# Seventh unit of layer one ahead of the sixth, bank copies ahead of casts, and narrowing in other steps

## The chip, the cores and the metric

The kernel runs on one core of a Trainium2 chip, in one launch. The metric is the device time of that launch in microseconds: 2001.27 is the median of three runs (1999.72 to 2001.92). TensorE (PE in the rows) multiplies, and loads its weights beside that (PEld). VectorE (DVE), ScalarE (ACT) and GpSimd (POOL) work on tiles, and the DMA queues are issued by SyncE (SP). Each engine runs its instructions in the order in which they stand.

## The reference

Windowed attention, a mixture of eight experts weighted by a Sinkhorn normalisation, and a second feed-forward layer, all in float32:

```python
x = attention(q, k, v)                       # 2304 tokens x 512
P = exp(x @ w_gate - max); 8 rounds of row and column normalisation
for e in range(8):                           # layer one, 1024 hidden units each
    h = np.maximum(x @ w1[e], 0.0)
    out += P[:, e:e + 1] * (h @ w2[e])
h = out @ w_in                               # layer two, 2048 hidden units
r = np.maximum(h, 0.0)
return (r * r) @ w_out
```

The weights w_in and w_out come as float64 bit patterns in int64 words and have to be made float32 on the chip; the kernel calls this narrowing.

## The kernel before

**Stages.** Attention and the Sinkhorn rounds come first. Then 80 steps, each with 256 hidden units: steps 0 to 31 are pass one over the experts (tokens 0 to 1023 as a pair of 512, with tokens 1024 to 1279 as a "single"), 32 to 63 are pass two over the experts (tokens 1280 to 2303), 64 to 71 and 72 to 79 the same two passes of layer two. Numbers are float32 split in a high part (a cast to float32r, on ScalarE) and a low part (the rest, a subtraction on VectorE); a product takes three matmuls, high by high, high by low and low by high.

**Units.** The pair of a step is multiplied in Strassen's manner. Layer one has seven units u1 to u7 of six matmuls of 512 columns (`l1_pair`, lines 683 to 799), in three banks: a (shown as s), b (pt) and c (xt). u1 fills a, and ScalarE copies it to b (line 759); u2 fills c; u3 adds into a and finishes block (0,0); u4 and u5 add into b, and ScalarE copies b to s2 and to s3 (lines 771 and 775). VectorE adds bank c into s3 (line 776), which finishes block (1,1). u6 adds into b and finishes (1,0). u7 adds into c; VectorE adds c into s2 (line 785), which finishes (0,1). Each block is scaled on VectorE (line 723) into r1 (0,0), r2 (1,1), r3 (1,0) and r4 (0,1), the last two in `mix32`. The second layer of a step is done in the step behind it (`l2_mixed`, lines 929 to 1001): 14 units v10 to v71 of three matmuls, from seven operands: "11" (from r1), "22" (r2), "21" (r3), and t1 to t4, which GpSimd makes by four subtractions from r1 to r4 (`mix`, line 737). `operand` (line 700) gives each its high part by a cast (line 702) and its low part by a subtraction (line 705). v1 reads "11", v2 "21", v6 t2, v3 "22", v7 t3, v4 t4, v5 t1; the last digit is a half of the output. Between these units ScalarE copies one bank into another (`copied`, line 967), and VectorE adds finished banks into `acc` (line 957). Pass one has besides us (24 matmuls of 256 columns) and w0, w1 for the single.

**Order.** Units are issued in the order of a string `names` in the main loop (line 1249 on); pass two runs "u1 v10+v11 u2 v20 u3 v60+v50 u4+cp v51+v30+v70 u5 v21+v61 u6 v40+v71+v31 u7 v41". Each item is one tick. `after(k, f)` (line 634) puts an instruction of the other engines k ticks later, behind what is already due there. So each engine's order is fixed by these ticks, and an instruction that waits holds up all behind it.

**Narrowing and splitting.** 32 pieces of 512 x 128 words; each is loaded by DMA (`load_raw`), goes through three stages on VectorE (`narrow`, lines 312 to 338: two, two and three instructions), and is stored. `work` holds the ticks behind which a stage is issued, `loads` those of a load without a stage. Pieces below DEEP = 7 are done in pass one, in steps 22 to 28, three stages a step; those below MID = 25 in pass two, two stages a step (ticks 6 and 12); the rest later. Splits (`split_on`, `blocks_of`) prepare the next pass's input in parts, one a step: a cast (line 360) and a subtraction on VectorE (line 363). Products of the second layer go through three banks "mm".

## Time and profile before

| | |
|---|---|
| median of three runs | 2001.27 us |
| the profiled execution's own time | 2000.11 us |
| its span, first to last instruction | 1998.3 us |
| TensorE busy | 1906.1 us (95%) |
| TensorE's weight loads busy | 1545.0 us (77%) |
| VectorE busy | 1648.7 us (83%) |
| ScalarE busy | 924.2 us (46%) |
| GpSimd busy | 789.5 us (40%) |
| mean granted clock of TensorE | 0.991 of 2.4 GHz |

Busy shares are means over stages that differ. Pass one lies from about 99 to 917 us, pass two to 1609, layer two behind it. In a timeline a row gives the start, the duration, the engine, the line, what is written and read, and in brackets how long the engine was idle before and what released it. A matmul's record is longer than the distance to the next one, since matmuls overlap.

### The profile page before, as it was taken

How to read it: one execution, taken by the hardware profiler on the slowest of the kernel's cores; microseconds unless marked ns; L12 is line 12 of the kernel's file. 1: busy time of each engine (PE TensorE's matmuls, PEld its weight loads, DVE VectorE, ACT ScalarE, POOL GpSimd, SP SyncE). 2: the span in 40 equal slices, each digit the busy share in tenths (PEclk: the TensorE clock that was granted, in tenths of full speed). 3: DMA queues.
4: the chain of work that ended last, by engine and by line, in shares of the span. 5: the costliest groups of instructions: out<-in, count | busy, mean ns of one | idle time of the engine just before them, and what ended most of it. 6: DMA issues, size and time to landing. Idle time of an engine off the chain costs nothing.

```text
span 1998.3 us, 28397 instructions
## 1 busy us (share of the span) xinstructions
PE 1906.1 (95%) x10247; PEld 1545.0 (77%) x10247; DVE 1648.7 (83%) x2344; ACT 924.2 (46%) x1568; POOL 789.5 (40%) x648
## 2 busy tenths in 40 slices
PE   8999999999999999999998999999899999999998
PEld 6678788888888777787777777777777778888777
DVE  6786799989999999987688888887778798875686
ACT  6744455545554444443433433433333466553544
POOL 3522466556655455452223323322322434421231
PEclk9999999999999999999999999999999999999999
DMA  8674676766666665659666876667555788879561
GB/s 294 232 280 156 235 240 231 246 240 237 232 249 222 206 231 190 221 213 393 252 256 210 297 262 242 231 254 253 217 214 196 286 332 328 310 285 381 212 233 64
DMA packets 166205, 492.78 MB, mean 247 GB/s; under 512 B 16992, under 2 KB 36336, under 8 KB 166064
## 3 DMA queue, kind: packets, MB, share of 16 engines
q1 hardware_dynamic: 166064, 490.96, 67.8%
q8 instruction: 81, 1.33, 0.3%
q14 instruction: 60, 0.49, 0.1%
HBM read 282.15 MB, written 208.74 MB: 246 GB/s over the span
## 4 chain that ended last, share of the span: by engine, by line
PE 42%; DVE 9%; POOL 3%; issue 2%; ACT 2%; POOLq 0%; ACTq 0%; DVEq 0%
PE pt L625 10%; PE mm L946 7%; PE s L946 7%; PE mm L849 6%; PE xt L625 4%; PE s L625 4%; POOL r L735 3%; DVE g L705 3%; PE xt L946 1%; PE mm L806 1%; DVE mix L723 1%; DVE s L785 1%; ACT s L968 1%; DVE acc L957 1%; ACT g L702 0%
## 5 line engine op out<-in xcount | busy, mean ns | idle before, releaser
L735 POOL TENSOR_TENSOR r<-mix,r 128x512 f32<-128x512 f32 x67 | 87.2, 1301 | 818.2 <-DVE mix L723 723.4
L705 DVE TENSOR_TENSOR g<-r,g 128x512 fp32r<-128x512 f32 x268 | 257.3, 961 | 91.7 <-ACT g L702 85.7
L946 PE MATMUL mm<-g,w2h 128*128 128x512 f32 x670 | 213.8, 401 | 49.4 <-ACT s L968 48.7
L702 ACT CAST g<-r 128x512 fp32r<-128x512 f32 x268 | 163.3, 620 | 209.5 <-POOL r L735 109.9
L946 PE MATMUL s<-g,mixh 128*128 128x512 f32 x670 | 216.1, 399 | 12.8 <-DVE g L705 12.1
L702 ACT CAST g<-mix 128x512 fp32r<-128x512 f32 x201 | 124.3, 620 | 176.4 <-DVE mix L723 88.4
L946 PEld LDWEIGHTS mm<-g,w2h 128*128 128x128 f32 x670 | 124.2, 190 | 88.2 <-ACT s L968 63.5
L957 DVE TENSOR_TENSOR acc<-mm,acc 128x512 f32<-128x512 f32 x260 | 177.0, 681 | 4.2 <-PE mm L946 4.1
L957 DVE TENSOR_TENSOR acc<-s,acc 128x512 f32<-128x512 f32 x260 | 174.3, 682 | 6.6 <-PE s L946 6.1
L946 PEld LDWEIGHTS s<-g,mixh 128*128 128x128 f32 x670 | 125.4, 189 | 54.3 <-DVE g L705 25.7
L705 DVE TENSOR_TENSOR g<-mix,g 128x512 fp32r<-128x512 f32 x201 | 150.7, 762 | 1.4
L946 PE MATMUL mm<-g,w2l 128*128 128x512 f32 x335 | 132.5, 396 | 0.0
L849 PE MATMUL mm<-w2h,g 128*128 128x512 f32 x416 | 129.8, 393 | 0.1
L625 PE MATMUL pt<-x_hi,sumh 128*128 128x512 f32 x316 | 127.4, 403 | 1.1 <-ACT s L771 0.7
L625 PE MATMUL s<-x_hi,blkh 128*128 128x512 f32 x316 | 126.1, 399 | 0.0
L625 PE MATMUL s<-x_lo,blkh 128*128 128x512 f32 x316 | 125.3, 397 | 0.0
L625 PE MATMUL s<-x_hi,blkl 128*128 128x512 f32 x316 | 125.0, 395 | 0.0
L625 PE MATMUL pt<-x_lo,sumh 128*128 128x512 f32 x316 | 124.6, 394 | 0.0
L625 PE MATMUL pt<-x_hi,suml 128*128 128x512 f32 x316 | 124.1, 393 | 0.0
L625 PE MATMUL xt<-x_hi,sumh 128*128 128x512 f32 x316 | 123.6, 391 | 0.3 <-DVE s L776 0.3
L625 PE MATMUL xt<-x_hi,suml 128*128 128x512 f32 x316 | 123.1, 389 | 0.0
L625 PE MATMUL xt<-x_lo,sumh 128*128 128x512 f32 x316 | 123.0, 389 | 0.0
(262 smaller groups left out, 4930.3 us busy)
## 6 DMA issues: line engine op xcount, KB each, us to landing
raw<-in_w SPq DMA_DIRECT2D x61, 512.0 KB, 4.1
w_blkh<-blkh SPq DMA_DIRECT2D x40, 512.0 KB, 5.1
w_blkl<-blkl SPq DMA_DIRECT2D x40, 512.0 KB, 5.8
w_sumh<-sumh SPq DMA_DIRECT2D x40, 512.0 KB, 5.3
w_suml<-suml SPq DMA_DIRECT2D x40, 512.0 KB, 4.5
w_w2h<-w2h SPq DMA_DIRECT2D x40, 512.0 KB, 6.3
w_w2l<-w2l SPq DMA_DIRECT2D x40, 512.0 KB, 6.3
blkh<-w_blkh SPq DMA_DIRECT2D x40, 512.0 KB, 4.8
```

The lines of the kernel that those rows point to most:

```text
L625: nc.tensor.matmul(ps, w[:, c], z[:, x, j], start=start and k == 0, stop=stop and k == 5, skip_group_check=True)
L702: after(k, lambda: nc.scalar.copy(b[:, 0], src))
L705: lambda: nc.vector.tensor_tensor(out=b[:, 1], in0=src, in1=b[:, 0].bitcast(F32), op=ALU.subtract),
L723: lambda: nc.vector.scalar_tensor_tensor(out=g, in0=src, scalar=0.0, in1=p, op0=ALU.max, op1=ALU.mult),
L735: sub = lambda o, x, y: nc.gpsimd.tensor_tensor(out=o, in0=x, in1=y, op=ALU.subtract)
L785: after(0, lambda: nc.vector.tensor_tensor(out=made["s2"], in0=bank_c, in1=made["s2"], op=ALU.add))
L806: nc.tensor.matmul(ps, w[:, c], z[:, kc], start=k == 0, stop=k == len(terms) - 1)
L849: nc.tensor.matmul(ps, g[:, c0 * 128:c0 * 128 + 128], wt[:, fc], start=k == 0, stop=k == 3 * FC - 1)
L946: nc.tensor.matmul(ps, w[wt][:, c], block[n][:, g], start=start and k == 0, stop=stop and k == 2, skip_group_check=True)
L957: nc.vector.tensor_tensor(out=o, in0=ps, in1=o, op=ALU.add)
L968: after(0, lambda: nc.scalar.copy(out, src))
```

## The change

u7 and u6 change places wherever the mixing operands of the next step hang on them, so that u7 stands directly behind v21+v61, and u6 two items later. The casts and subtractions that follow are given other ticks: t1 now comes before t2, "21" and "22" later, and the subtraction r3 - r5 is issued on its own behind u6. v50 comes before v60. `copied` puts the bank copy first among what is due in its tick, not last. Narrowing: three pieces in steps 3 and 4, none in steps 22 to 28, and in pass two 22 pieces instead of 18, with two buffers in turn, at ticks 4 and 8, or 4, 6 and 8 where nothing is split. The splits of pass one move from steps 4 to 19 to steps 6 to 21. Of the table of orders two lines are shown, and of the diff what the text speaks of.

```diff
@@ -44,7 +44,7 @@
 NEG = -1e30
 NWARM = 9
 TURN = 4
-DEEP = 7
+DEEP = 3
 MID = 25
 
 
@@ -288,7 +288,7 @@
             return
         asked[0] += 1
         which, s, k = raw_pieces[n]
-        z = deep[0] if n < DEEP else raw2 if n < MID else apart[0]
+        z = deep[0] if n < DEEP else (raw2, acc[1])[n % 2] if n < MID else apart[0]
         src = loaded[n] = z.bitcast(I32).rearrange("p (n w) -> p n w", w=2)
         nc.sync.dma_start(
             src.rearrange("p n w -> p (n w)"),
@@ -728,9 +728,10 @@
                 k += 2 if i <= NS1 else 1
                 operand("11", g, k, k + 1)
             elif (fc, t) == (1, 1):
-                operand("22", g, *((7, 8) if i + 1 in first else (5, 6) if i < NS1 else (4, 5)))
+                operand("22", g, *((7, 8) if i + 1 in first else (6, 7)))
             elif (fc, t) == (1, 0):
-                operand("21", g, k + 1, k + 2 if moe else k + 3)
+                operand("21", g, 2, 3)
+                after(4, lambda: nc.gpsimd.tensor_tensor(out=r3, in0=r3, in1=r5, op=ALU.subtract))
             else:
                 sub = lambda o, x, y: nc.gpsimd.tensor_tensor(out=o, in0=x, in1=y, op=ALU.subtract)
 
@@ -738,12 +739,11 @@
                     sub(r1, r4, r1)
                     sub(r5, r2, r1)
                     sub(r4, r2, r4)
-                    sub(r3, r3, r5)
 
                 after(2, mix)
-                t1, t2, t3, t4 = ((3, 4), (4, 5), (5, 7), (6, 8)) if i >= NS1 else ((5, 7), (5, 6), (6, 9), (7, 11))
+                t1, t2, t3, t4 = ((4, 5), (5, 6), (6, 7), (8, 9)) if i >= NS1 else ((6, 7), (7, 8), (8, 10), (11, 13))
+                operand("t1", r1, *t1)
                 operand("t2", r5, *t2)
-                operand("t1", r1, *t1)
                 operand("t3", r4, *t3)
                 operand("t4", r3, *t4)
 
@@ -778,14 +778,14 @@
 
         def u6():
             product(bank_b, i, "blk", 3, 3, stop=True)
-            out(1, 0, bank_b, 1 if steps[i][0] and mixed(i) else 0)
+            out(1, 0, bank_b, 0)
+            if steps[i][0] and steps[i][1] % SPE == SPE - 1:
+                after(1, lambda: load_p(pair_of(i), steps[i][1] // SPE + 1, 1))
 
         def u7():
             product(bank_c, i, "sum", 3, 2, stop=True)
             after(0, lambda: nc.vector.tensor_tensor(out=made["s2"], in0=bank_c, in1=made["s2"], op=ALU.add))
             out(0, 1, made["s2"], 1 if mixed(i) else 2)
-            if steps[i][0] and steps[i][1] % SPE == SPE - 1:
-                after(1, lambda: load_p(pair_of(i), steps[i][1] // SPE + 1, 1))
 
         def results():
             made_here()
@@ -965,7 +965,7 @@
             after(0, f)
 
         def copied(out, src):
-            after(0, lambda: nc.scalar.copy(out, src))
+            due.setdefault(clock[0], []).insert(0, lambda: nc.scalar.copy(out, src))
 
         def chain(m, b1, b2, b3, p):
             def v1():
@@ -1249,18 +1249,20 @@
...
                 elif i < NS1:
-                    names = "u1 v10 u2 v20 w0 u3 v60+v50+v11 u4+cp v51+v30+v70 u5 v21+v61 u6 v40+v71+v31 w1 u7 v41 us"
+                    names = "u1 v10 u2 v20 w0 u3 v50+v60+v11 u4+cp v51+v30+v70 u5 v21+v61 u7 w1 v40+v71+v31 u6 v41 us"
                 else:
-                    names = "u1 v10+v11 u2 v20 u3 v60+v50 u4+cp v51+v30+v70 u5 v21+v61 u6 v40+v71+v31 u7 v41"
+                    names = "u1 v10+v11 u2 v20 u3 v50+v60 u4+cp v51+v30+v70 u5 v21+v61 u7 v40+v71+v31 u6 v41"
@@ -1268,10 +1270,10 @@
                 order = [together([(u | v)[n] for n in item.split("+")]) for item in names.split()]
                 l2, l2s, l1s, ahead = [], [], [], []
             elif i == TURN:
-                order = l2[:5] + l2s + l1[:4] + [u for k in range(3) for u in (l2[5 + k], l1[4 + k])]
+                order = l2[:5] + l2s + l1[:4] + [u for k, n in ((5, 4), (6, 6), (7, 5)) for u in (l2[k], l1[n])]
                 l2, l2s = [], []
             else:
-                for u in l1[4:]:
+                for u in (l1[4], l1[6], l1[5]) if i == first[3] else l1[4:]:
                     order += l2[:1] + [u]
                     l2 = l2[1:]
             order += l2 + l2s + l1s
@@ -1293,15 +1295,15 @@
                 splits.append(blocks_of(1, y_dram[:, :, :2 * T], y0 + raw))
             if i == 2 * NS1 - 1:
                 apart[:] = xb(), post[0].tile([128, T], F32, tag="pp", name="pp", bufs=3)
-            if i == TURN:
+            if i in (SCALED - 1, SCALED):
+                deep.append(xb())
+            if i == TURN + 2:
                 y = two(xb()) + two(xb())
                 splits.append(blocks_of(0, x_dram, y + two(mixes[0][0])))
-            if i == TURN + 17:
-                deep[:] = xb(), xb()
             if i == 2 * NS1 + 1:
                 y1 = two(mix32) + tuple(post[0].tile([128, T], F32, tag="pp", name="pp", bufs=3) for _ in range(2))
                 splits.append(blocks_of(2, y_dram[:, :, PAIRS[1]:], y1 + two(mixes[0][0]) + two(xb().bitcast(F32R))))
-            if TURN <= i < TURN + 16:
+            if TURN + 2 <= i < TURN + 18:
                 split_on(0, 8, 9)
             elif NS1 + 4 <= i < 2 * NS1 - 4:
                 split_on(1, 5, 9)
@@ -1312,10 +1314,13 @@
                 for k, f in enumerate(operands_single()):
                     after(8 + 2 * k, f)
             work, loads = (), ()
-            if TURN + 17 <= i < NS1 - 1 and done[0] < DEEP:
-                work, loads = ((), (2,)) if i == TURN + 17 else ((1, 8, 14), ())
-            elif NS1 < i < 2 * NS1 - 3 and done[0] < MID:
-                work, loads = ((), (2,)) if i == NS1 + 1 else ((6, 12), ())
+            if i == SCALED - 1:
+                loads = (3,)
+            elif SCALED <= i <= TURN:
+                work = (1, 4, 7) if i == SCALED else (1, 4, 7, 13, 15, 17)
+            elif NS1 <= i < 2 * NS1 - 3:
+                work = () if i == NS1 else (4, 8) if NS1 + 4 <= i < NS1 + 20 else (4, 6, 8)
+                loads = (15, 17) if i == NS1 else ()
             elif 2 * NS1 - 1 <= i < first[3] - 1 and done[0] < len(raw_pieces):
                 work = () if i == 2 * NS1 - 1 else (2, 4, 6)
                 loads = (8,)
```

The order that comes out in a pass-two step, first on ScalarE, around the copy from v10's bank (L968 "s<-mm"); L702 are the casts of r1 to r5, and L759 is u1's copy. In the kernel before r_2749, r_2750 and r_2751 are r1, r2 and r5, and mix_1878 holds r3 and r4. Before:

```order
L968 COPY s<-s 128x512
L702 CAST g_1875<-r_2750 128x512
L702 CAST g_1875<-mix_1878 128x512
L759 COPY pt<-s 128x512
L702 CAST g_1875<-r_2749 128x512
L968 COPY s<-mm 128x512
L702 CAST g_1876<-r_2751 128x512
L702 CAST g_1876<-mix_1878 128x512 x2
```

After; r1, r2 and r5 are r_2764, r_2765 and r_2766:

```order
L968 COPY s<-s 128x512
L702 CAST g_1875<-r_2765 128x512
L702 CAST g_1875<-r_2764 128x512
L702 CAST g_1875<-mix_1878 128x512
L759 COPY pt<-s 128x512
L968 COPY s<-mm 128x512
L702 CAST g_1876<-r_2766 128x512
L702 CAST g_1876<-mix_1878 128x512 x2
```

The cast of t1 (from r1) has moved from between the two copies to ahead of u1's copy.

On VectorE, the stretch up to the addition of s3 (L776) in a pass-two step with a split; L957 are additions into acc, L313 and L317 a first stage of narrowing, L363 a split's subtraction. Before:

```order
L705 TENSOR_TENSOR g_1876<-mix_1878,g_1876 128x512 x2
L705 TENSOR_TENSOR g_1875<-r_2749,g_1875 128x512
L313 TENSOR_SCALAR sums<-raw_113 128x512
L317 SCALAR_TENSOR_TENSOR sums<-raw_113,sums 128x512
L957 TENSOR_TENSOR acc_1873<-s,acc_1873 128x512
L957 TENSOR_TENSOR acc_1873<-mm,acc_1873 128x512
L363 TENSOR_TENSOR raw_111<-xb,raw_111 128x512
L776 TENSOR_TENSOR s_152<-xt,s_152 128x512
```

After, in which acc_1874 is the second buffer of loads:

```order
L705 TENSOR_TENSOR g_1876<-mix_1878,g_1876 128x512
L705 TENSOR_TENSOR g_1875<-r_2764,g_1875 128x512
L957 TENSOR_TENSOR acc_1873<-s,acc_1873 128x512
L957 TENSOR_TENSOR acc_1873<-mm,acc_1873 128x512
L313 TENSOR_SCALAR sums<-acc_1874 128x512
L317 SCALAR_TENSOR_TENSOR sums<-acc_1874,sums 128x512
L363 TENSOR_TENSOR raw_111<-xb,raw_111 128x512
L776 TENSOR_TENSOR s_152<-xt,s_152 128x512
```

The stage of narrowing has moved from ahead of the two additions to between them and L776.

## Rows read from the trace of the kernel before

**Rows 1.** Windows: start:end, length, each engine's busy us, clock, DMA share, GB/s.

```profile
159.00:214.80 55.80, 55.80 (x286) 47.03 (x285) 32.96 (x45) 27.39 (x41) 10.15 (x12) 1.00 0.57 195
...
617.10:642.10 25.00, 24.99 (x123) 20.85 (x123) 21.38 (x29) 12.04 (x19) 14.01 (x13) 1.00 0.66 232
667.50:867.50 200.00, 184.96 (x843) 148.44 (x842) 189.81 (x242) 85.49 (x133) 99.87 (x85) 0.97 0.62 214
917.40:1006.50 89.10, 82.89 (x355) 66.34 (x354) 61.35 (x88) 36.46 (x65) 20.49 (x14) 0.98 0.78 297
1006.50:1350.40 343.90, 317.07 (x1345) 251.30 (x1344) 288.03 (x425) 132.98 (x238) 106.94 (x72) 0.99 0.69 252
1350.40:1567.40 217.00, 199.60 (x842) 159.82 (x841) 173.38 (x256) 78.88 (x140) 59.39 (x40) 0.98 0.64 235
1567.40:1587.30 19.90, 19.51 (x85) 15.60 (x84) 15.71 (x23) 8.79 (x15) 5.97 (x4) 1.00 0.43 162
```

**Rows 2.** Waits of TensorE: who waited, for whom, total us, times, longest.

```profile
PE mm L946 <- ACT s L968: 48.7, 31, 2.2
...
PE mm L806 <- DVE acc L875: 1.9, 8, 0.3
```

**Rows 3.** Timeline, pass two, from u7's end to v20: start, duration, engine, line.

```profile
1091.09 0.69 DVE L785 TENSOR_TENSOR s<-xt,s 128x512 f32<-128x512 f32 x1 [0.67 <-PE xt L625]
...
1091.70 0.42 DVE L330 TENSOR_SCALAR raw<-sums 128x512 int32<-128x512 int32 x1
...
1092.88 0.69 DVE L336 TENSOR_TENSOR sums<-sums,raw 128x512 f32<-128x512 f32 x1
...
1094.69 0.68 DVE L723 SCALAR_TENSOR_TENSOR mix<-s,pp 128x512 f32<-128x512 f32 x1
...
1095.52 1.27 POOL L735 TENSOR_TENSOR r<-mix,r 128x512 f32<-128x512 f32 x1 [9.12 <-DVE mix L723]
...
1096.82 0.62 ACT L702 CAST g<-r 128x512 fp32r<-128x512 f32 x1 [3.12 <-POOL r L735]
...
1097.35 0.58 ACT L968 COPY s<-mm 128x512 f32<-128x512 f32 x1
1097.47 2.88 DVE L705 TENSOR_TENSOR g<-r,g 128x512 fp32r<-128x512 f32 x2 [1.49 <-ACT g L702]
...
1097.98 1.22 PE L946 MATMUL mm<-g,w2h 128*128 128x512 f32 x2 [2.17 <-ACT s L968]
```

**Rows 4.** Timeline, pass one, step 23: a stage of narrowing, then what follows it.

```profile
672.49 1.39 DVE L313 TENSOR_SCALAR xb<-xb 128x512 int32<-128x512 int32 x1 [0.70 <-DMA xb<-in_w_in]
...
675.51 1.21 DVE L705 TENSOR_TENSOR g<-r,g 128x512 fp32r<-128x512 f32 x1
...
676.77 0.50 PE L946 MATMUL s<-g,mixh 128*128 128x512 f32 x1 [1.66 <-DVE g L705]
```

**Rows 5.** Timeline, pass two, step 40: up to u6's first matmul.

```profile
1104.25 0.42 DVE L313 TENSOR_SCALAR sums<-raw 128x512 int32<-128x512 int32 x1
...
1104.71 0.69 DVE L317 SCALAR_TENSOR_TENSOR sums<-raw,sums 128x512 int32<-128x512 int32 x1
...
1106.64 0.69 DVE L957 TENSOR_TENSOR acc<-mm,acc 128x512 f32<-128x512 f32 x1
...
1107.25 0.68 DVE L363 TENSOR_TENSOR raw<-xb,raw 128x512 fp32r<-128x512 f32 x1
...
1108.62 0.69 DVE L776 TENSOR_TENSOR s<-xt,s 128x512 f32<-128x512 f32 x1 [0.69 <-ACT s L775]
...
1109.16 0.39 PE L625 MATMUL pt<-x_hi,blkh 128*128 128x512 f32 x1
```

**Rows 6.** Timeline, pass one, step 13, with a split: up to u6's first matmul.

```profile
431.06 0.85 DVE L363 TENSOR_TENSOR mixh<-xb,mixh 128x512 fp32r<-128x512 f32 x1
...
431.84 0.68 DVE L776 TENSOR_TENSOR s<-xt,s 128x512 f32<-128x512 f32 x1
431.99 0.39 PE L625 MATMUL pt<-x_hi,blkh 128*128 128x512 f32 x1
```

More of the change, by code (lines that the diff above doesn't have):

```diff
@@ L1251, in tile_kernel @@
                 if i == first[2]:
-                    names = "v10 u1 v20 us v60+v50 v51+v30 v70 u2 v11 u3 v40 u4+cp v21+v61 u5 v71+v31 u6 v41 u7"
+                    names = "v10 u1 v20 us v50+v60 v51+v30 v70 u2 v11 u3 v40 u4+cp v21+v61 u5 v71+v31 u6 v41 u7"
                 elif i == NS1:
                     u |= zip(("w0", "w1"), l2s)
-                    names = "v10 u1 v20 w0 v60+v50 w1 v51+v30 u2 v11 u3 v70 u4+cp v21+v61 u5 v40+v71+v31 u6 v41 u7"
+                    names = "v10 u1 v20 w0 v50+v60 w1 v51+v30 u2 v11 u3 v70 u4+cp v21+v61 u5 v40+v71+v31 u7 v41 u6"
                 elif i == first[1] - 1:
-                    names = "u1 v10 u2 v20 w0 u3 v11 u4 v60+v50+cp u5 v51+v30+v70 u6 v21+v61 u7 w1 v40+v71+v31 us v41"
-                elif i in (first[2] - 1, len(steps) - 1):
-                    names = "u1 v10+v11 u2 v20 u3 u4 v60+v50+cp u5 v51+v30+v70 u6 v21+v61 u7 v71+v40+v31 v41"
+                    names = "u1 v10 u2 v20 w0 u3 v11 u4 v50+v60+cp u5 v51+v30+v70 u7 v21+v61 u6 w1 v40+v71+v31 us v41"
+                elif i == first[2] - 1:
+                    names = "u1 v10+v11 u2 v20 u3 u4 v50+v60+cp u5 v51+v30+v70 u7 v21+v61 u6 v71+v40+v31 v41"
+                elif i == len(steps) - 1:
+                    names = "u1 v10+v11 u2 v20 u3 u4 v50+v60+cp u5 v51+v30+v70 u6 v21+v61 u7 v71+v40+v31 v41"
                 elif i < NS1:
-                    names = "u1 v10 u2 v20 w0 u3 v60+v50+v11 u4+cp v51+v30+v70 u5 v21+v61 u6 v40+v71+v31 w1 u7 v41 us"
+                    names = "u1 v10 u2 v20 w0 u3 v50+v60+v11 u4+cp v51+v30+v70 u5 v21+v61 u7 w1 v40+v71+v31 u6 v41 us"
                 else:
-                    names = "u1 v10+v11 u2 v20 u3 v60+v50 u4+cp v51+v30+v70 u5 v21+v61 u6 v40+v71+v31 u7 v41"
+                    names = "u1 v10+v11 u2 v20 u3 v50+v60 u4+cp v51+v30+v70 u5 v21+v61 u7 v40+v71+v31 u6 v41"
                 def together(fs):
```

## The prediction, made before the changed kernel had run

> **What bounds the kernel now.** I read the table of engines first: TensorE is busy 95% of the span, so time can be won only where it waits or runs at its lower clock. Then the windows [rows 1], cut where steps begin (at a step's first matmul of u1). A pass-one step that neither narrows nor splits takes 25.00 us and TensorE is busy for all of it. The seven steps from 667.5 us, in which layer-two weights are narrowed, take 200.0 us, 28.6 each, at a mean granted clock of 0.97 instead of 1.00, so part of them ran at 1.2 GHz. In pass two sixteen steps take 343.9 us (21.49 each) and the next ten 217.0 us (21.70 each), while the step at 1567.4 us, which narrows nothing, takes 19.90.
>
> Third, the waits [rows 2]: the largest of TensorE is 48.7 us, 31 times, for a ScalarE copy of line 968. Fourth, the timeline around one such wait [rows 3]. u7's result is added at 1091.09; the narrowing that follows u7 runs on VectorE from 1091.70 to 1093.57; only then come two low parts and the scaling (1094.69), GpSimd's subtraction (1095.52), ScalarE's cast of t1 (1096.82), and behind it in ScalarE's order the copy (1097.35 to 1097.93). v20 overwrites the bank that this copy reads, so it starts at 1097.98, after 2.17 us of idle. The copy had nothing to wait for but its place in the queue: its source was v10's bank, finished two units before.
>
> The floor of a pass-two step: 19.90 less 0.39 of idle (busy 19.51) [rows 1], less some 0.16, because a matmul's record is 0.39 us long while the next starts after about 19.9 / 85 = 0.23, so a short wait shows less idle than it costs. That gives 19.35.
>
> A sentence of the Trainium skill bears on this reading (Perfetto Trace Analysis, Identifying the Most-Contended Engine): matmul occupancy is a poor measure of headroom, and the busy share of weight loads a better one. By matmul occupancy the sixteen steps could gain 343.9 - 317.1 = 27 us; by weight loads, brought from 251.3 / 343.9 = 0.73 to the 0.83 of the clean pass-one step, 43 us, which is close to what the step times give (343.9 - 16 x 19.35 = 34); the trace sides with the page, and the sum below goes by step times.
>
> **The change part by part.**
>
> *Narrowing leaves steps 22 to 28.* The cause of the loss there is in [rows 4]: a first stage waits 0.70 us for its DMA with VectorE's whole queue behind it, its first instruction takes 1.39 us (0.42 in [rows 5]), the low part behind it ends at 676.72, and TensorE starts at 676.77 after 1.66 us of idle. The delay shows one step after the narrowing, hence the window from step 23. After the change these steps hold neither narrowing nor splits (which end at step 21), so I give them the clean 25.00: 200.0 - 7 x 25.0 = **-25.0 us**. What is late next there is u7, priced below.
>
> *Three pieces go into steps 3 and 4.* Nine stages, 1.15 us each in lines 313 and 317 [rows 5] or 1.87 for a third stage [rows 3]. In that stretch VectorE is busy for 33.0 of 55.8 us and TensorE for all of it [rows 1]; banks of products are three deep, and that covers a stage. Lower bound 0; upper, the price that the 21 stages had in pass one, 25.0 / 21 = 1.2 each, 10.7. In step 4 u7 also comes one pair of units after u5, and step 5 inherits third-stage work in front of its low parts. I take **+4**, nearer the idle VectorE than the full one.
>
> *u7 ahead of u6.* u7 adds into the bank that u5's sum s3 is read from, so it must wait for VectorE's add of line 776; u6 needed only ScalarE's copy before it. Its new place is where u6 began. In a pass-one step with a split the add runs 431.84 to 432.52 and u6 began at 431.99 [rows 6]: 0.53 late, plus 0.05 from release to matmul as in [rows 3] (1097.93 to 1097.98), about 0.6. There are 14 such steps: +8.4. Without the split's subtraction (line 363, 0.78 from its start to the add's) VectorE is ready in time, and what is left is the copy of s3 and the add behind it: 1109.31 against 1109.16 [rows 5], 0.2. Twelve steps: +2.4. In exchange w1 comes directly behind u7 and its add no longer holds the single's bank: 8 waits of 1.9 us in all [rows 2], each 0.16 more in truth, -3.2. Together **+7.6**. Behind the waiting u7 on TensorE stand w1, v40, v71, v31 and u6, all of which move with it; nobody else waits longer.
>
> The gain of the same swap: the mixing starts two units, 15 matmuls or 3.4 us, earlier, and u6's own product r3 is taken out of the chain (its subtraction moves behind the others). "21" now comes after u6, at the end of the step, and is wanted at v20: in pass two five units later, with VectorE's queue waiting there for TensorE; no cost.
>
> *Bank copies ahead of casts, and no narrowing behind u7, in pass two.* Casts of 22, t1 and 21 still stand ahead of v10's copy. t1 is ready 3.4 us sooner by the swap and 1.9 us sooner by the stage that no longer follows u7: 5.3 us against a wait of 2.17 [rows 3]. The cast of 21 needs u6, which ends one v unit and u1 before v10: 2 us for an add of 0.7 and a cast of 0.6. So the wait at v20 goes. The cover of the casts that now stand behind the copy (t2, t3) is u2, v20 and u3, 3.4 us, against 0.6 us of copy; without it each step would pay 0.6.
>
> *What is late next in pass two: u7 again.* Narrowing now stands at places 4 and 8 (steps 36 to 51) or 4, 6 and 8 (33 to 35 and 52 to 60), and place 8 is right in front of line 776 on VectorE. In [rows 5] v70's addition ends at 1107.33; a first or second stage (1.15) makes 1108.4, line 363 (0.6 net of overlap) 1109.0, the add 1109.7: 0.55 late with the release. A third stage (1.87) makes it 1.25. One stage in three is a third: mean 0.78. With three stages the split's subtraction is gone, but two stages stand ahead of v70's addition; I take the same 0.78. Bounds: 0.2, if VectorE gets ahead, and 1.5. So 25 steps x (19.35 + 0.78) + 19.55 for step 61 = 522.8 against 343.9 + 217.0 = 560.9: **-38.1 us**. The extra four pieces cost VectorE some 16 us, spread over a stretch where it is idle for 344 - 288 us; two buffers instead of one take the loads off its path.
>
> *Steps 32 to 35*: 89.1 us; step 32 has twelve matmuls more, so the floor is 4 x 19.35 + 2.7 = 80.1, and three steps narrow (0.78 each): up to -6.6, of which I take **-4**, since the turning transposes of step 32 stay. *Second pass of layer two*: seven steps at 0.2 for u7, less what the earlier mixing returns: **+1**.
>
> Sum: -25.0 + 4 + 7.6 - 38.1 - 4 + 1 = -54.5. The profiled execution took 2000.11 us, so 1945.6; the median of the runs is 1.2 us above it, so **1946 us** in round numbers.
>
> **The rivals.**
>
> *VectorE gets ahead in pass two.* Steps no longer stretched by stalls could leave it earlier at v70's addition, or stages overlap better. For: it idles 0.69 us before line 776 now [rows 5]. Against: v70's addition waits for TensorE, so its end is fixed. u7 then waits 0.2: 25 x 0.58 = 14.5 us less, 1932.
>
> *GpSimd and VectorE collide before v20 in pass one.* The mixing now runs beside the wide low parts and the low part of "21". Beside GpSimd's subtractions two low parts took 2.88 us [rows 3], where one alone takes some 0.7. From u7's end to v20 TensorE has 39 full matmuls and 24 half ones, 11.6 us; VectorE has ten operations of 0.62 and two wide ones of 1.2 to 2, about 9.3. Three stretched by 0.8 each use that up, and wide ones stretched too leave v20 0.5 to 1.5 us late: 26 steps, +13 to +39, 1959 to 1985. By the Trainium skill (SBUF — State Buffer, two separate sides) a VectorE operation with two SBUF inputs and a GpSimd operation that reads SBUF shut each other out for a whole instruction; by that rule the stretch would be a full subtraction, 1.3 to 1.7 us, and this rival the likelier, while 2.88 for two lies below two full exclusions.
>
> *Slower: u7 becomes the new bottleneck everywhere.* Without u7's waits the other terms come to about -86 us; u7 stands ahead of u6 in some 66 steps, so from 1.3 us per step the change loses. The price that could do it is a third stage and a split ahead of line 776 (1.25) plus matmuls at the lower clock after it, about 1.7: 66 x 1.7 - 86 = +26, 2027. Against: most steps have no third stage at place 8, pass one none at all.
>
> *The copy does not act*: something ahead of it in ScalarE's queue still waits, say the cast of 21. Pass two then keeps its 21.5 us, and -25 + 4 + 7.6 + 1 leaves 1989.
>
> **How the numbers follow.** Forecast (1934 to 1960) 0.63; VectorE ahead 0.15; collision 0.12; copy without effect 0.06; slower 0.04. The range for 8 in 10 takes in the forecast, the first rival down to 1926 and the cheap half of the collision, to 1970. Within 0.2% (4 us, about what a measurement of this kernel can tell from no change) only a mixture falls, 0.01; slower by more 0.04; faster by more 0.95.
>
> **What would show it.** Windows of steps 23 to 29 near 25 us each; no wait at line 968 in pass two; in its place TensorE waiting for VectorE's line 776 at the xt product of u7, 0.2 to 1.3 us a step, longest behind third stages and in pass one only with splits; granted clock 1.00 in pass two. Wrong it would be by a wait at v20 for a low part in pass one, by u7's wait over 1.3, or by steps 3 to 5 growing by more than 10 us.

## The result and the profile after

The changed kernel takes 1944.89 us (median of four runs, 1944.12 to 1945.29) against 2000.56 for the kernel before beside it: a ratio of 0.9721, with a 95% interval of 0.9704 to 0.9737. The forecast was 1946 us, in a range of 1926 to 1970. The profiled execution has a span of 1943.5 us where that of before had 1998.3. The table of engines:

```profile
PE 1888.3 (97%) x10247; PEld 1539.0 (79%) x10247; DVE 1651.7 (85%) x2344; ACT 925.2 (48%) x1568; POOL 755.1 (39%) x648
```

The windows of the changed kernel, cut again where steps begin. Columns: start and end, length, busy time (and count) of TensorE, its weight loads, VectorE, ScalarE and GpSimd, granted clock, DMA share, GB/s. In the order of the rows they are steps 3 and 4, step 22, steps 23 to 29, 32 to 35, 36 to 51, 52 to 61 and step 62; the last row is steps 6 to 21:

```profile
159.00:215.80 56.80, 55.36 (x283) 46.49 (x282) 41.94 (x60) 26.09 (x39) 11.80 (x14) 1.00 0.57 200
659.00:684.60 25.60, 25.18 (x122) 20.68 (x121) 22.90 (x29) 12.20 (x19) 13.51 (x13) 1.00 0.57 205
684.60:863.90 179.30, 176.34 (x842) 144.71 (x841) 160.28 (x197) 85.41 (x133) 94.64 (x85) 1.00 0.60 211
914.90:1002.90 88.00, 82.78 (x355) 66.34 (x354) 67.89 (x103) 35.91 (x65) 18.38 (x14) 0.98 0.85 322
1002.90:1320.70 317.80, 309.76 (x1346) 251.06 (x1345) 290.48 (x425) 134.54 (x238) 101.29 (x73) 1.00 0.73 273
1320.70:1516.00 195.30, 193.38 (x842) 156.92 (x841) 181.13 (x270) 79.53 (x140) 55.35 (x41) 1.00 0.69 261
1516.00:1535.40 19.40, 19.36 (x85) 15.56 (x84) 15.97 (x23) 8.83 (x15) 5.09 (x5) 1.00 0.56 217
...
246.90:659.00 412.10, 402.71 (x1922) 330.73 (x1921) 377.03 (x463) 202.55 (x318) 234.30 (x201) 1.00 0.65 232
```

Against [rows 1]: the seven steps from 23 fell from 200.0 to 179.3 us, the sixteen from 36 from 343.9 to 317.8, and the granted clock of both is 1.00 now. But a pass-one step that narrows and splits nothing takes 25.60 (step 22) where it took 25.00, and steps 6 to 21 take 25.76 each (412.10 / 16). TensorE is no longer busy for all of them.

The waits of TensorE (who, for whom, total us, times, longest), against [rows 2]:

```profile
PE xt L625 <- DVE s L776: 17.7, 43, 1.4
PE s L946 <- DVE acc L957: 10.7, 27, 0.8
PE mm L946 <- DVE g L705: 5.4, 3, 3.0
```

Of the 31 waits for the copy of line 968 one of 0.5 us is left, in step 32. In their place stands u7 behind VectorE's add of line 776, as forecast, and a wait that no part of the prediction names: a second-layer product into bank "s", behind an addition of line 957, 27 times. In the kernel before it occurred twice:

```profile
PE s L946 <- DVE acc L957: 1.4, 2, 0.8
```

**u7 in pass two.** VectorE in step 41, up to u7's first matmul (start, duration, engine, line; in brackets the idle time before and what ended it):

```profile
1112.85 0.69 DVE L957 TENSOR_TENSOR acc<-mm,acc 128x512 f32<-128x512 f32 x1
1113.46 0.42 DVE L330 TENSOR_SCALAR acc<-sums 128x512 int32<-128x512 int32 x1
...
1114.64 0.69 DVE L336 TENSOR_TENSOR sums<-sums,acc 128x512 f32<-128x512 f32 x1
1115.25 0.69 DVE L363 TENSOR_TENSOR raw<-xb,raw 128x512 fp32r<-128x512 f32 x1
1115.85 0.68 DVE L776 TENSOR_TENSOR s<-xt,s 128x512 f32<-128x512 f32 x1
...
1116.59 0.50 PE L625 MATMUL xt<-x_hi,sumh 128*128 128x512 f32 x1 [1.06 <-DVE s L776]
```

v70's addition, then a third stage (1113.46 to 1115.33), the split's subtraction and the add: the order in which the prediction put them. u7 starts 1.45 us after the matmul before it, where 0.23 is usual, so the step loses 1.22; with a first or second stage (step 40) the distance is 0.72 and the loss 0.49.

Why v20 doesn't wait any more: the cast of t1 starts 2.9 us after u7's add (line 787, from 1118.30) in the same step, and the copy and v20 follow in the next:

```profile
1121.19 0.62 ACT L702 CAST g<-r 128x512 fp32r<-128x512 f32 x1 [0.16 <-POOL r L736]
...
1124.44 0.57 ACT L968 COPY s<-mm 128x512 f32<-128x512 f32 x1
...
1126.28 0.61 PE L946 MATMUL mm<-g,w2h 128*128 128x512 f32 x2
```

The cast of t1 ends 2.6 us ahead of the copy, where in [rows 3] it ended at the copy's start with v20 waiting behind both.

**The new wait in pass one.** Step 14, from u7's addition to v41. v41's first half goes into bank "s" again, which the last addition here still reads:

```profile
469.83 0.69 DVE L787 TENSOR_TENSOR s<-xt,s 128x512 f32<-128x512 f32 x1 [0.51 <-PE xt L625]
...
471.19 0.75 DVE L875 SCALAR_TENSOR_TENSOR acc<-mm,ptile,acc 128x512 f32<-128x512 f32 x1 [0.67 <-PE mm L849]
...
471.86 1.22 DVE L178 TENSOR_TENSOR suml<-sums,sumh 128x1024 fp32r<-128x1024 f32 x1
...
472.99 0.69 DVE L723 SCALAR_TENSOR_TENSOR mix<-s,pp 128x512 f32<-128x512 f32 x1
...
473.59 0.68 DVE L957 TENSOR_TENSOR acc<-mm,acc 128x512 f32<-128x512 f32 x1
...
474.19 1.28 DVE L957 TENSOR_TENSOR acc<-s,acc 128x512 f32<-128x512 f32 x2
...
474.93 0.73 PE L946 MATMUL s<-g,w2h 128*128 128x512 f32 x2 [0.38 <-DVE acc L957]
```

w1 stands directly behind u7 now. Its addition (line 875) waits for its product; behind it in VectorE's order stand the wide low part of the next step's sums (1.22), the scaling of u7's block, the addition of v40, and only then that of v71, which frees the bank. Before, w1 and u7 stood behind v71 and ahead of v41, so their work on VectorE came later than that addition.

**Step 5.** One long wait is left there, behind a third stage that stands at place 17 of step 4. VectorE (and one instruction of GpSimd) up to v20, and v20:

```profile
216.50 0.92 DVE L330 TENSOR_SCALAR xb<-xb 128x512 int32<-128x512 int32 x1
...
217.46 1.67 DVE L333 SCALAR_TENSOR_TENSOR xb<-xb 128x512 f32<-128x512 uint32 x1
...
218.54 1.18 POOL L192 TENSOR_TENSOR sums<-raw 128x256 f32<-128x256 f32 x1
...
219.16 1.11 DVE L336 TENSOR_TENSOR xb<-xb 128x512 f32<-128x512 f32 x1
...
221.39 1.21 DVE L705 TENSOR_TENSOR g<-mix,g 128x512 fp32r<-128x512 f32 x1
...
222.65 0.50 PE L946 MATMUL mm<-g,w2h 128*128 128x512 f32 x1 [2.96 <-DVE g L705]
```

The stage takes 3.77 us from 216.50 to 220.27, beside subtractions of GpSimd, against 1.87 in pass two [rows 3], and the low part of "21" (221.39 to 222.60) follows two other operations. Step 5 takes 31.0 us where it took 27.2.

### The profile page after: what moved, and what is told of

Read it like the earlier page. It is cut to its first block, busy times and chain, and to the rows that moved or that the text cites. A ratio compares the mean times of both kernels' runs of the same rounds, so it can differ in the third digit from the quotient of the medians.

```text
span 1943.5 us, 28331 instructions
## 1 busy us (share of the span) xinstructions
PE 1888.3 (97%) x10247; PEld 1539.0 (79%) x10247; DVE 1651.7 (85%) x2344; ACT 925.2 (48%) x1568; POOL 755.1 (39%) x648
## 4 chain that ended last, share of the span: by engine, by line
PE 64%; DVE 26%; issue 4%; ACT 3%; DMA 2%; POOL 0%; SPq 0%; DVEq 0%; ACTq 0%; POOLq 0%
PE mm L849 11%; PE xt L625 10%; PE pt L625 9%; PE mm L946 9%; PE s L625 8%; PE s L946 8%; DVE acc L957 6%; DVE g L705 5%; PE mm L806 3%; DVE s L776 2%; DVE mixl L178 2%; PE xt L946 2%; DVE suml L178 2%; DVE mix L723 1%; DVE blkl L178 1%
## 5 line engine op out<-in xcount | busy, mean ns | idle before, releaser
L705 DVE TENSOR_TENSOR g<-r,g 128x512 fp32r<-128x512 f32 x268 | 253.3, 964 | 25.1 <-ACT g L702 23.8
L702 ACT CAST g<-r 128x512 fp32r<-128x512 f32 x268 | 165.3, 621 | 113.5 <-DVE acc L957 52.8
L946 PE MATMUL mm<-g,w2h 128*128 128x512 f32 x670 | 208.1, 391 | 7.8 <-DVE g L705 5.4
L946 PE MATMUL s<-g,mixh 128*128 128x512 f32 x670 | 206.9, 390 | 0.0
L705 DVE TENSOR_TENSOR g<-mix,g 128x512 fp32r<-128x512 f32 x201 | 190.9, 950 | 3.0 <-ACT g L702 3.0
L957 DVE TENSOR_TENSOR acc<-s,acc 128x512 f32<-128x512 f32 x260 | 172.8, 684 | 11.3 <-PE s L946 11.2
L957 DVE TENSOR_TENSOR acc<-mm,acc 128x512 f32<-128x512 f32 x260 | 177.3, 682 | 0.2 <-PE mm L946 0.2
L702 ACT CAST g<-mix 128x512 fp32r<-128x512 f32 x201 | 124.5, 620 | 107.8 <-DVE mix L723 58.6
L625 PE MATMUL xt<-x_hi,sumh 128*128 128x512 f32 x316 | 130.9, 414 | 18.7 <-DVE s L776 17.7
L246 POOL TENSOR_TENSOR raw<-raw 128x256 f32<-128x256 f32 x36 | 38.2, 1060 | 273.6 <-DVE w2l L178 249.2
L734 POOL TENSOR_TENSOR mix<-mix,r 128x512 f32<-128x512 f32 x67 | 103.0, 1538 | 95.7 <-DVE g L705 95.7
L625 PE MATMUL pt<-x_hi,sumh 128*128 128x512 f32 x316 | 123.1, 389 | 0.0
```

What stands on the lines that cost most here:

```text
L246: tt(out=r[:, 1, 1], in0=r[:, 0, 1], in1=r[:, 1, 1], op=ALU.add)
L625: nc.tensor.matmul(ps, w[:, c], z[:, x, j], start=start and k == 0, stop=stop and k == 5, skip_group_check=True)
L702: after(k, lambda: nc.scalar.copy(b[:, 0], src))
L705: lambda: nc.vector.tensor_tensor(out=b[:, 1], in0=src, in1=b[:, 0].bitcast(F32), op=ALU.subtract),
L734: after(4, lambda: nc.gpsimd.tensor_tensor(out=r3, in0=r3, in1=r5, op=ALU.subtract))
L946: nc.tensor.matmul(ps, w[wt][:, c], block[n][:, g], start=start and k == 0, stop=stop and k == 2, skip_group_check=True)
```

## Experiments

All ratios are to the kernel before, run beside it on the same chip, each from at least four runs. Lengths of steps come from one profiled execution each.

**Narrowing alone.** From the kernel before, only the narrowing and its splits and buffers are moved as in the change:

```diff
-DEEP = 7
+DEEP = 3
...
-            if TURN <= i < TURN + 16:
+            if TURN + 2 <= i < TURN + 18:
...
-            if TURN + 17 <= i < NS1 - 1 and done[0] < DEEP:
-                work, loads = ((), (2,)) if i == TURN + 17 else ((1, 8, 14), ())
...
+            elif SCALED <= i <= TURN:
+                work = (1, 4, 7) if i == SCALED else (1, 4, 7, 13, 15, 17)
+            elif NS1 <= i < 2 * NS1 - 3:
+                work = () if i == NS1 else (4, 8) if NS1 + 4 <= i < NS1 + 20 else (4, 6, 8)
```

> The kernel before with the narrowing moved as in the change (three pieces in steps 3 and 4, 22 in pass two with two buffers at ticks 4, 8 or 4, 6, 8, splits two steps later); u6 ahead of u7, bank copies last. Theory 1 (the loss at v20 in pass two is mostly the stage of narrowing that followed u7 on VectorE, not the order of u6 and u7): the wait at v20 falls to about 0.4 us a step as in the step at 1567 us of the kernel before, a pass-two step takes 19.6 to 20.0, steps 23 to 29 take 25.0, v41 and the xt product of u7 wait for nothing; 1932 to 1944. Theory 2 (the swap is what takes the wait at v20 away): over 1.0 us a step stays at v20, steps of 20.7 or more, 1960 to 1975.

1934.07 us, ratio 0.968 [0.9664, 0.9697]: faster than the whole change. Its windows of steps 23 to 29 and 36 to 51, and its largest wait:

```profile
674.30:847.20 172.90, 172.89 (x843) 145.69 (x842) 149.21 (x197) 84.30 (x133) 97.61 (x85) 1.00 0.62 219
...
983.60:1306.00 322.40, 315.80 (x1346) 248.61 (x1346) 284.53 (x425) 132.77 (x238) 106.82 (x72) 1.00 0.74 269
```

```profile
PE mm L946 <- ACT s L968: 13.9, 31, 1.9
```

A pass-one step without narrowing or splits takes 24.70, and in pass two v20's wait falls from 48.7 us in all to 13.9 (0.4 a step), although u6 is ahead of u7 and the copies are last. That it is the stage behind u7 shows in the wait of the kernel before: 1.46 us in two steps of three and 2.16 in the third, a difference of 0.70, as a third stage (1.87) takes 0.72 longer than the others (1.15). So the narrowing is worth more than the whole, and the rest of the change costs 8 us by the ratios and 13 by the lengths of the steps. (In this kernel's profiled execution the stretch ahead of step 1, which no edit touches, took 104.5 us; in the others 98.5 to 101.9.)

**The swap alone** (u7 ahead of u6, with its ticks and names; narrowing and copies as before):

```diff
-                operand("21", g, k + 1, k + 2 if moe else k + 3)
+                operand("21", g, 2, 3)
+                after(4, lambda: nc.gpsimd.tensor_tensor(out=r3, in0=r3, in1=r5, op=ALU.subtract))
...
-                    names = "u1 v10+v11 u2 v20 u3 v60+v50 u4+cp v51+v30+v70 u5 v21+v61 u6 v40+v71+v31 u7 v41"
+                    names = "u1 v10+v11 u2 v20 u3 v50+v60 u4+cp v51+v30+v70 u5 v21+v61 u7 v40+v71+v31 u6 v41"
```

> The kernel before with u7 ahead of u6 and the ticks that belong to it alone; narrowing and bank copies as before. Theory 1: v20's wait in pass two goes too, since t1 is ready 3.4 us sooner, and a step there takes about 19.6; pass one keeps its narrowing in steps 22 to 28 (28 us a step or more) and gains a wait of 0.5 us a step at v41, for v71's addition behind the wide low part of the sums; 1960 to 1975. Theory 2 says the same for pass two, and no loss in pass one: 1945 to 1958.

1985.55 us, ratio 0.9938 [0.9924, 0.9953]: less gain than any theory gave it. Its waits:

```profile
PE xt L625 <- DVE s L776: 15.5, 20, 1.5
PE mm L946 <- DVE g L705: 14.9, 36, 1.2
PE s L946 <- DVE acc L957: 10.7, 27, 0.8
```

Pass two wins (20.25 a step in steps 36 to 51, from 21.49), but steps 6 to 22 take 25.93 instead of 25.03, and the steps that still narrow in pass one grow to 29.56. In step 25 a low part, line 875, the copy of line 771, the add of line 776 and v41 are all waited for, one after the other. The wait of line 957 is here with the same total as in the whole change, so it belongs to the swap.

**Bank copies first alone, and with the narrowing.**

```diff
         def copied(out, src):
-            after(0, lambda: nc.scalar.copy(out, src))
+            due.setdefault(clock[0], []).insert(0, lambda: nc.scalar.copy(out, src))
```

> The kernel before with the bank copies first in their tick, and nothing else. Theory 1: the wait at v20 goes, but t1's cast now stands behind the copy and VectorE's low parts are as late as before, so v60 and v50 wait for a low part instead, 0.5 to 1.2 us a step in pass two; pass one is as before; 1970 to 1992. Rival (the place of the copy in ScalarE's queue was the whole loss of pass two): steps of 19.6, 1950 to 1958.

> Narrowing moved and bank copies first, u6 ahead of u7 as before. Theory 1: nothing waits at v20, v60 waits for t2's low part by less than 0.5 us, and pass one has neither v41's wait nor u7's; 1928 to 1938, faster than the whole change. Theory 2 (the swap is needed): v60 or v50 wait 1 us or more a step, 1950 to 1970.

Alone 1991.6 us, 0.9964 [0.9952, 0.9977]; with the narrowing 1936.68, 0.9694 [0.968, 0.9708], no better than the narrowing alone. The largest wait with the copies alone:

```profile
PE s L946 <- DVE g L705: 43.0, 44, 1.7
```

The copy gets out earlier (11.3 us of the wait for it are left) and most of the wait moves to v60, for the low part of t2: the mixing was late as such, and the copy's place in ScalarE's queue mainly decided which unit shows it.

**The whole change with the copies last again** (the edit above, undone).

> The changed kernel with the bank copies last in their tick, as before. Theory 1 (once t1 is early, what stands ahead of the copy has been ready for long, and its place is worth little): v20 waits 0.1 us or less, 1943 to 1950. Rival (the copies' place is what frees v20 in pass two): a wait at v20 of 0.5 us or more in each of 30 steps, 1960 to 1990.

1945.8 us, 0.9737 [0.9723, 0.9752], beside 0.9721 [0.9704, 0.9737] for the whole change, with the same 19.86 in steps 36 to 51. With t1 ready 2.6 us ahead of the copy, its order there decides nothing.

**The wide low part one place earlier in pass one**, out of v71's way:

```diff
-            at = (8, 9, 12, 16) if n == 2 * NS1 else (2, 5, 10, 12) if TURN + 1 < n < NS1 else (2, 5, 10, 14) if n < NS1 else (2, 5, 8, 11)
+            at = (8, 9, 12, 16) if n == 2 * NS1 else (2, 5, 10, 11) if TURN + 1 < n < NS1 else (2, 5, 10, 14) if n < NS1 else (2, 5, 8, 11)
```

> The changed kernel with one number altered: in pass one the low part of the sums (a wide VectorE operation of 1.2 us or more) is issued one tick earlier, with u7 and not with w1. Theory 1 (in pass one v41 waits because this operation and then r4's scaling stand ahead of v71's addition, whose bank v41 overwrites): the wait at v41, 0.54 us of lost start and 0.1 behind it in each of 27 steps, falls below 0.2 us, a step takes 25.0 to 25.2 instead of 25.7, 1929 to 1935. Rival (VectorE is simply short of time in pass one): steps stay at 25.5 or more, 1941 to 1947.

1940.07 us, 0.9709 [0.9694, 0.9723]. The wait:

```profile
PE s L946 <- DVE acc L957: 3.9, 9, 0.8
```

It falls to a third, and steps 6 to 22 and 23 to 29 take 25.56 and 25.31 instead of 25.75 and 25.61: the low part is a cause, but only a third of the gain that was expected comes. In steps 22 to 30 v41's matmul still starts 0.43 to 0.47 us after the one before it, and u7's 0.43: VectorE, with the scaling and v40's addition in front of v71's, stays just behind.

**No stage right ahead of line 776 in pass two:**

```diff
-                work = () if i == NS1 else (4, 8) if NS1 + 4 <= i < NS1 + 20 else (4, 6, 8)
+                work = () if i == NS1 else (4, 6) if NS1 + 4 <= i < NS1 + 20 else (2, 4, 6)
```

> The changed kernel with the narrowing of pass two at ticks 4 and 6 in place of 4 and 8, and 2, 4 and 6 in place of 4, 6 and 8. Theory 1 (in pass two u7 waits for the addition of s3 only because a stage of narrowing stands right in front of it): the wait falls to what the copy and the addition take, 0.2 us, a step takes 19.4, 1933 to 1939. Rival (VectorE's queue there is late by its sum, wherever the stage stands): u7 waits as before, 1943 to 1947.

1940.24 us, 0.9707 [0.9693, 0.9722]; steps 36 to 51 take 19.51 instead of 19.86, steps 52 to 60 the same 19.51. The wait:

```profile
PE xt L625 <- DVE s L776: 11.2, 32, 1.4
```

So the stage cost 0.35 a step where it stood at place 8 with a split behind it, 5.6 us in sixteen steps. In most of these steps 0.2 is left of u7's wait (0.43 between the matmuls instead of 0.23), for the copy of s3 and the add themselves. Every third step, with a third stage at place 6, still shows 0.90, so there it is more than these two, and the time came out 1.2 us above the 1933 to 1939 that were expected.

**The swap from step 32 on only.** Steps 4 to 31 get u6 first and the ticks of before, everything else is the changed kernel:

```diff
-                operand("21", g, 2, 3)
-                after(4, lambda: nc.gpsimd.tensor_tensor(out=r3, in0=r3, in1=r5, op=ALU.subtract))
+                if i < NS1:
+                    operand("21", g, k + 1, k + 2)
+                else:
+                    operand("21", g, 2, 3)
+                    after(4, lambda: nc.gpsimd.tensor_tensor(out=r3, in0=r3, in1=r5, op=ALU.subtract))
...
                 elif i < NS1:
-                    names = "u1 v10 u2 v20 w0 u3 v50+v60+v11 u4+cp v51+v30+v70 u5 v21+v61 u7 w1 v40+v71+v31 u6 v41 us"
+                    names = "u1 v10 u2 v20 w0 u3 v60+v50+v11 u4+cp v51+v30+v70 u5 v21+v61 u6 v40+v71+v31 w1 u7 v41 us"
```

> The changed kernel with u6 ahead of u7 and the ticks of before in pass one (steps 4 to 31), and u7 ahead of u6 from step 32 on; copies first and narrowing as in the change. Theory 1 (the swap costs 0.7 us a step in pass one, where the wide low parts stand on VectorE, and is worth 0.3 to 0.5 us a step in pass two): pass-one steps of 24.6 to 25.1, pass-two steps of 19.5 to 20.4, 1919 to 1927. Rival (the two orders hang together, or the swap is worth nothing in pass two): 1932 or more.

1926.25 us, 0.9636 [0.962, 0.9652], faster than both kernels. Steps 4 to 31 take 20.7 us less than in the changed kernel, and nothing behind them changes by over 1 us.

**Both of the last two** (the swap from step 32 on, narrowing at 4 and 6 or 2, 4 and 6).

> Pass one's steps 4 to 31 with u6 ahead of u7 and the ticks of before, the rest as changed; and the narrowing of pass two at places 4 and 6 (with splits) or 2, 4 and 6, so that no stage stands right ahead of line 776. Theory: the two losses are independent, so the 5.6 us that the places gave in the sixteen steps with splits come off the 1926.25 us of the kernel with pass one put back: 1919 to 1922, those steps at 19.5 each and pass one unchanged. Rival: with pass one put back another wait takes the place in pass two, and the time stays at 1925 to 1927.

1921.09 us, 0.9614 [0.96, 0.9628]. Its windows of steps 6 to 22, 23 to 29 and 36 to 51:

```profile
248.60:674.10 425.50, 423.63 (x2042) 352.48 (x2041) 389.01 (x491) 215.67 (x337) 258.32 (x213) 1.00 0.67 237
674.10:848.40 174.30, 174.09 (x843) 145.62 (x842) 152.12 (x197) 85.51 (x133) 97.38 (x85) 1.00 0.63 217
...
986.90:1299.00 312.10, 309.50 (x1345) 251.00 (x1344) 288.07 (x425) 134.51 (x238) 100.99 (x73) 1.00 0.75 278
```

The two losses are independent: the sixteen steps from 36 give the same 5.6 us as in the changed kernel, and pass one keeps its gain.

**Three attempts at what is left.** The narrowing of step 4 moved forward into step 3; the same with step 32 in the old order and ticks; and, instead, one piece in each of steps 3, 4 and 5:

```diff
-                work = (1, 4, 7) if i == SCALED else (1, 4, 7, 13, 15, 17)
+                work = (1, 4, 7, 11, 13, 15) if i == SCALED else (1, 4, 7)
```

```diff
-                    names = "v10 u1 v20 w0 v50+v60 w1 v51+v30 u2 v11 u3 v70 u4+cp v21+v61 u5 v40+v71+v31 u7 v41 u6"
+                    names = "v10 u1 v20 w0 v60+v50 w1 v51+v30 u2 v11 u3 v70 u4+cp v21+v61 u5 v40+v71+v31 u6 v41 u7"
```

```diff
-            elif SCALED <= i <= TURN:
-                work = (1, 4, 7) if i == SCALED else (1, 4, 7, 13, 15, 17)
+            elif SCALED <= i <= TURN + 1 and done[0] < DEEP:
+                work = (1, 4, 7)
```

> As the kernel with both (pass one put back, places 4 and 6), and the narrowing of steps 3 and 4 put at other places: step 3 at 1, 4, 7, 11, 13 and 15, step 4 at 1, 4 and 7 alone, so that no stage stands at the end of step 4. Theory: the wait of some 2.8 us at v20 of step 5 comes from the stages at places 13 to 17 of step 4, ahead of the low part of 21; then step 5 falls from 29.3 to 27.2, step 4 may grow by 0.5 to 1, and the time is 1 to 2 us below the kernel with both: 1917 to 1920. Rival: the low part of 21 is late in step 5 for the order of the mixing in step 4 whatever narrows, and the time doesn't change by more than 0.5.

> As the kernel before in this list, and step 32 (the turn of the passes) with u6 ahead of u7 and the ticks of before too, so that the swap acts from step 33 on. Theory: the two waits at v20 of step 33 (0.97 and 1.38 us of idle in the changed kernel, with matmuls at the lower clock behind them) come from 21, which is made last when u6 ends step 32; then step 33 falls by 1.5 to 2.5 us and step 32 stays within 0.5: 1 to 2.5 us less than without it, 1915 to 1918. Rival: step 32 without the swap gets back the wait for the first operand t1 (2.17 us of idle a step in the kernel before), and nothing is won, within 0.7.

> As the kernel with both (pass one put back, places 4 and 6 in pass two), and the narrowing's first three pieces one to a step, in steps 3, 4 and 5, each at places 1, 4 and 7, so that no stage stands at the end of steps 3 and 4, where it cost a wait at v20 of step 5 (stages at 13 to 17 of step 4) or two of the single's products in step 3 (stages at 11 to 15 of step 3). Theory: the price lies in the place and not in the piece; steps 3, 4 and 5 take 37.9, 18 and 26.5 to 27.5 (37.9, 18.4 and 30.5 in the kernel with both), and the time is 3 to 4 us below that of the kernel with both, leaving aside that the stretch ahead of step 1 varies by some 3 us between runs. Rival: a stage at 7 of step 5 is as dear as elsewhere in pass one (1.2 us each for the 21 stages of the kernel before), and step 5 stays above 29.

1924.72 us (0.9634 [0.962, 0.9648]), 1926.55 (0.9642 [0.9623, 0.9661]) and 1920.87 (0.9614 [0.9598, 0.963]). In the first, step 5 falls from 30.5 to 26.2 us as expected, but step 3 grows from 37.9 to 45.0: the stages at its end hold the single's additions (line 886 there), for which TensorE waits 1.67 and 2.38 us. In the second, v20's waits in step 33 are gone, one of 3.91 us for the low part of t1 stands at v50 of the same step, so that step takes 25.96 us instead of 23.95, and step 32 takes the same 25.2; nothing was won, as the rival said. In the third, steps 3, 4 and 5 take 37.9, 17.9 and 27.7, 3.3 us less than with both (step 5 was to end at 27.5), but the median doesn't follow. In that execution step 32 took 1.7 us more: behind the same wait of 1.87 us at v20 the granted clock was 0.60 for 4.3 us, where it was 1.00 in the kernel with both. Why it fell in the one and not in the other is open. By the lengths of these steps the price of a stage lies in its place.

## Why the prediction was right, and where it wasn't

The total was met within 1.1 us, but only because errors of some ten microseconds cancel. By its own terms, lengths of steps in the trace of before and after, and of the narrowing alone where that separates a term:

| term | forecast | measured |
|---|---|---|
| narrowing leaves steps 22 to 28 (steps 23 to 29) | -25.0 | -27.1 (narrowing alone: 200.0 to 172.9) |
| three pieces into steps 3 and 4 (steps 3 to 5) | +4 | +1.9 alone, +5.4 with the swap |
| u7 ahead in pass one, from step 6 on | +7.6 | +20.1 (changed kernel less narrowing alone, steps 6 to 31) |
| pass two, steps 36 to 61 | -38.1 | -47.8 |
| steps 32 to 35 | -4 | -1.1 |
| end of pass two, steps 62 and 63 | not in the sum | -2.5 |
| layer two (steps 64 to 78) | +1 | 0.0 (its second pass +0.6, its first -0.6) |
| sum | -54.5 | -53.0 of the 54.8 between the two profiled executions |

*Narrowing leaves pass one: right.* The clean step is 24.70 in the kernel with the narrowing alone, not 25.00; why the row that I took as clean [rows 1] was 0.3 longer stays open. (With the copies first it is 24.88, in the kernel with the narrowing and the copies.)

*u7 in pass one: the step that failed.* The prediction said of what stands behind u7 on TensorE that all of it moves along and "nobody else waits longer". It followed TensorE's order and not VectorE's: with w1 directly behind u7, its addition and the wide low part come between u7's add and the addition that v41 waits for. That wait stands in the trace 27 times (10.7 us of idle, 0.54 lost each time, since the matmul starts 0.77 us after the one before). u7's own wait was no larger than forecast: 0.4 lost in the fourteen steps with a split, against 0.6, and 0.2 in the others. The bank wait of line 806 that was to go is gone. Moving the low part takes the wait away in two thirds of the steps but gives only 5.3 us in steps 6 to 29, so the low part is shown as one cause, and the rest of VectorE's queue behind u7 (scaling and v40's addition) is argued. That the cost belongs to the swap is shown: with the copies last in both kernels, steps 6 to 31 take 668.7 us with it and 647.9 without, 20.8 more. With the copies first in both it is 18.2 (668.0 against 649.8), since without the swap they cost 2.0 us there. The 20.7 us that return with u6 first in steps 4 to 31 are 17.8 in steps 6 to 31 and 2.8 in steps 4 and 5.

*Pass two: right in mechanism, 9.7 us too small.* The waits of u7 have the sizes of the sum (0.49 and 1.22 lost, against 0.55 and 1.25) where a split is made. Mis-sized were two numbers. Without a split (steps 52 to 60) I took the same 0.78, but there a step shows 0.62 between the matmuls instead of 0.23, so 0.39 lost; and the floor of 19.35 was too high: the step from 1516.00, which narrows nothing, takes 19.40 with u7's wait of 0.2 in it, so 19.2. Together that is 25 x 0.15 + 9 x 0.39 = 7.3 of the 9.7.

*What the gain belongs to: not what I said.* I put the whole of -38.1 down to swap, copies and narrowing together and named the copy's place in the queue as the cause of v20's wait. What decided was when t1 is ready. The copies are worth nothing beside either of the other two. The narrowing alone gives 39.2 us of the 47.8 in steps 36 to 61; the swap adds 8.6 there and 2.5 in steps 62 and 63, and costs more than that in pass one. The swap alone would give 33.9 in steps 36 to 61 (560.9 to 527.0), so the two largely do the same work, and most of the gain can't be put down to one of them alone. That the copy does not act was a rival, at 1989 us; it holds for the copy, but its price does not, since the swap and the narrowing do its work. Of the three measures of headroom in the sixteen steps from 36 (27 us by matmul occupancy, 43 by weight loads, 34 by step times) the one by step times lies nearest to what the best kernel here won, 343.9 - 312.1 = 31.8, and to what the floor of 19.2 would give, 36.7. By the Trainium skill (Perfetto Trace Analysis, Identifying the Most-Contended Engine) weight loads are the better measure of the other two; here they gave too much and occupancy too little, and which of the two lies nearer depends on whether one takes 31.8 or 36.7. So the trace does not side with the page as clearly as the prediction said.

*The other rivals.* That u7 turns the sign needed 1.3 us a step; in pass one the swap cost 20.1 / 26 = 0.8, so this rival had the place of the loss and not its price. VectorE ahead in pass two: in step 40 it still waits for TensorE ahead of v30's and v70's additions (0.37 us, 0.56 before), so their end is fixed as the prediction said; the places 4 and 6 bring what this rival promised, in part. The collision of GpSimd and VectorE before v20 shows in steps 5, 33 and 73 only, three waits of 5.4 us together, in step 5 with the stretched stage above. By the Trainium skill (SBUF — State Buffer, two separate sides) a two-input VectorE operation and a GpSimd operation that reads SBUF exclude each other; the stretched operations there (1.67 for line 333, where it takes 0.69 in step 41) go in that direction. In pass one as a whole it didn't decide: from step 6 on v20 doesn't wait. Of the three signs of being wrong, two occurred, but each in single steps only: the wait at v20 for a low part in pass one (2.96 us in step 5), and u7's wait over 1.3 us (1.44 in step 4, 1.38 in step 72). Steps 3 to 5 grew by 5.4 us, not by more than 10.

## What to carry to other kernels

An edit that moves a unit on the engine that bounds the kernel moves the instructions that it issues on all the others; follow each of those queues from the moved instruction to the next one that frees a bank, not only the units of the bounding engine. Change only the stage where the wait is: beside the moved narrowing the same swap gained 11 us in steps 36 to 63 and lost 21 in steps 6 to 31, and a table of orders by stage costs nothing. And where a wait names an instruction that had nothing to wait for but its queue, look at why the instructions ahead of it in that queue are late: the copy stood behind a cast that came late because narrowing followed u7 on VectorE, and taking that narrowing away did what the copies' new order could not.

## What the runs showed of the chip

A wait can cost more than its idle time, because in some cases TensorE's clock falls after it. In the kernel before, the wait of 2.17 us in [rows 3] is followed by a stretch at half the clock; so is the wait of 2.96 us in step 5 of the changed kernel; behind the one of 1.06 us in step 41 it stays up. The length of a wait doesn't decide it alone: behind the wait of 2.16 us in step 43 of the kernel before the clock stays up too. Of nine such waits in steps 37 to 61 five are followed by a fall (these steps take 23.0 to 23.1 us) and four are not (21.7 to 21.9); behind the waits of 1.46 us in the steps between it never falls. What decides is open. Windows right behind the four waits, two of the kernel before first (steps 40 and 43), then two of the changed one:

```profile
1097.90:1101.00 3.10, 3.02 (x7) 2.47 (x8) 2.92 (x3) 1.27 (x3) 3.10 (x3) 0.50 0.69 84
1163.20:1166.30 3.10, 2.99 (x12) 2.28 (x13) 2.96 (x4) 1.30 (x3) 3.10 (x3) 1.00 0.88 357
```

```profile
222.60:228.20 5.60, 5.55 (x17) 4.45 (x18) 4.51 (x6) 0.00 (x0) 2.27 (x2) 0.70 0.00 0
...
1116.50:1122.00 5.50, 5.41 (x24) 4.45 (x25) 4.69 (x9) 1.25 (x2) 2.06 (x2) 1.00 0.77 216
```

A granted clock of 0.50 is the level of 1.2 GHz, and matmuls then follow each other at 0.43 us instead of 0.23. A step with such a fall takes 1.2 us more than one with the same wait and none. Five of them make 6 us, and that is part of why the loss in pass two (560.9 us for 26 steps with a floor of 19.2, so 61.7) was larger than the 44.2 us of v20's wait in these steps, and why the shorter wait with the narrowing alone gave back more (39.2 us) than the idle time that it saved (33.8).
